# Attention, a Fourier mix and a feed-forward layer on one core: last group's sums on VectorE, last mirrored rows by an indirect store, the first row of weights in two halves of tokens, some conversions moved

## The chip, the cores and the metric

The kernel runs on one core of one Trainium2 chip. The core has engines that run their own streams of instructions in order and meet at semaphores: TensorE (PE; its weight loads are listed as PEld), VectorE (DVE), ScalarE (ACT), GpSimd (POOL) and SyncE (SP), which in this kernel only issues DMAs. ACT and POOL can issue DMAs too. Times are device microseconds of the whole execution; the metric is the median of several runs. The profile is of one execution.

## The reference

There are eight batches of 576 tokens, with eight heads of 64 numbers, so 512 numbers a token. Per batch: an attention in which the softmax of q runs over the 64 numbers of a head and the softmax of k over the tokens, then a Fourier mix, a layer norm without scale or shift, and a feed-forward layer.

```
q_s = softmax(q, over the head's numbers);  k_s = softmax(k, over the tokens)
kv  = einsum('bhsd,bhse->bhde', k_s, v);    x = einsum('bhsd,bhde->bhse', q_s, kv), heads side by side
u   = x + real(fft(fft(x, over tokens), over the 512 numbers))
un  = (u - mean(u)) / sqrt(var(u) + 1e-6)
out = u + relu(un @ w_ch1) @ w_ch2            # 512 -> 2048 -> 512
```

All is fp32. The inputs w_ch1 and w_ch2 are handed to the kernel as they are, seen as 64-bit words.

## The kernel before, in words

**Groups.** The tokens of a batch are cut in four tiles of 128, which the code names (c, u), c and u being 0 or 1; `tokens(c, u)` gives their rows. Tiles with c different from u are held in reversed order (token n and its mirror image n' are folded together for the Fourier transform, which is done by matmuls). The 64 tokens of a batch that are left over are put together over the batches in one more group, the shared one. So there are nine groups of 512 tokens, run in the order 0 to 6, the shared one, then batch 7, which is the *last group*. The place in this order is called `order`, 0 to 8.

**The feed-forward layer.** `plain` does group 0 by ordinary matmuls: `up(f)` (L1160) computes one *row* of 128 of the 2048 hidden numbers from the normalised tokens `unT` and row f of the first weights, `relu(f)` (ACT, L1165) follows, and then `part` (L1172) multiplies into the outputs. The other groups use Strassen's seven products: `up` (L1234) with its combinations `plus` (L1204: `u2` and `u3`), `other` (L1245, L1246) and `a_side` (L383 to L386, three sums of 128x512 on POOL per pair of rows), then from order 2 on `deep_down`, in which products are split once more: `a_step` (L1306) makes the combinations of the hidden tiles of a unit of two products (three on VectorE, the fourth, o = 6, on POOL), `product` (L1360) the matmuls, `ends` (L1367 and others) puts them together with temporaries `s1`, `u2`, `u3`, `into` and `sums` (L1310, L1313, POOL) add results to x, and `single` (L1330) with `add` (L1341) does products without a split. In the last group a single product, unit 4, comes at the very end and its two halves c = 0 and 1 are added to x one after the other.

**Words to weights.** The weights come as pairs of 32-bit halves, and each row of 128x512 is put together on the core by `convert(i)`: ACT scales the high half into a PSUM bank (L375), VectorE shifts it (L369) and sets the sign (L372), ACT scales the low half (L376), POOL adds (L377). Word i is row i of the first weights for i under 16, of the second after that. The banks are `bc`, `bb`, `bc`, `bb` for words 0 to 3, and `acc` later; `ba`, `bb` and `bc` are also the banks in which `up` accumulates its rows.

**Queries.** `q_exp` takes the maximum (L760), the exponential with its reduction (L766), the sum (L783), a small constant (L784), the reciprocal (L785) and scales (L794, VectorE); `q_turn` transposes on TensorE (L822) and ACT copies to qT (L832); `q_times_kv` multiplies (L884) and ACT copies the result to x (L901). The leftover tokens of two batches make a query tile of their own, named "t". `norm` normalises (L1096 on VectorE, L1099 on ACT), transposes (L1105) and copies to unT (L1114).

**Order of the work.** It is written by hand. Every step carries a planned time; all steps are sorted by it and issued in that order under a manual schedule, and each engine runs what it got in that order. The opening, up to the first normalised tokens, is a table of such times (OPENING), with WARM for products on TensorE that compute nothing that is used (L241). `first` = 46.9 is where row 0 starts in planned time. From order 1 on planned times are multiplied by 0.87. A planned time is a place in the order, not a moment in the execution.

**Stores.** `store` writes a tile of 128 tokens, or with d given one half of its 512 columns, to the output: with c equal to u by a direct DMA (L1482); with c different from u (the reversed tiles) in two steps, to a scratch tile in DRAM (L1489) and `wait` planned units later from there to the output in reversed order of rows, by pieces of 64 numbers (L1491, 256 bytes). Whole tiles and those with c = 1 leave by SP's queue, half tiles with c = 0 by ACT's.

## Time and profile before

| what | us |
|---|---|
| median of 3 runs (lowest to highest) | 1080.59 (1079.89 to 1081.19) |
| the profiled execution, whole | 1081.36 |
| its span on the core | 1079.6 |
| TensorE busy | 1059.0 |
| VectorE busy | 666.7 |
| GpSimd busy | 459.9 |
| ScalarE busy | 403.4 |
| first matmul of row 0 (L1160) starts | 51.33 |
| first matmul of row 1 starts | 55.28 |
| last matmul (L1330) ends | 1072.0 |
| last sum (L1341) starts | 1072.02 |
| last store (L1482 on SP's queue) is issued | 1072.47 |

The granted TensorE clock is 0.996 of full speed in the mean. Lines such as "PE bb L1160" name the engine, the tile written and the line of the kernel. In the list of waits the three numbers are microseconds in all, times, and the longest one. In the timeline each line is a run of like instructions: start, length from the first's start to the last's end, engine, line, operation, tiles written and read, how many, and in brackets how long the engine stood idle before and who ended it. "SPq" and "ACTq" are the DMA-issuing instructions of SP and ACT.

The sums on POOL by group of instructions: L383 (the first of the three in `a_side`) runs 32 times at 1278 ns, L1310 (`into`) 52 times at 1317 ns, L1306 on POOL 26 times at 1594 ns; L1306 on VectorE runs 92 times at 944 ns.

### The profile page before, as it was taken

How to read it: one execution, taken by the hardware profiler on the slowest of the kernel's cores; microseconds unless marked ns; L12 is line 12 of the kernel's file. 1: busy time of each engine (PE TensorE's matmuls, PEld its weight loads, DVE VectorE, ACT ScalarE, POOL GpSimd, SP SyncE). 2: the span in 40 equal slices, each digit the busy share in tenths (PEclk: the TensorE clock that was granted, in tenths of full speed). 3: DMA queues.
4: the chain of work that ended last, by engine and by line, in shares of the span. 5: the costliest groups of instructions: out<-in, count | busy, mean ns of one | idle time of the engine just before them, and what ended most of it. 6: DMA issues, size and time to landing. Idle time of an engine off the chain costs nothing.

```text
span 1079.6 us, 16993 instructions
## 1 busy us (share of the span) xinstructions
PE 1059.0 (98%) x6390; PEld 920.7 (85%) x6390; DVE 666.7 (62%) x1288; ACT 403.4 (37%) x953; POOL 459.9 (43%) x377
## 2 busy tenths in 40 slices
PE   8999999999999999999999999999999999999997
PEld 7744555988898899889998998889988998899896
DVE  6887787675545774677555765687457742562251
ACT  4675533542245215531453234522552132131200
POOL 3162220165512733454515443374236443553343
PEclk9999999999999999999999999999999999999999
DMA  9487569548976576646755577547644664665473
GB/s 338 160 283 253 176 227 308 184 171 272 341 253 206 191 254 231 223 175 200 271 177 188 195 245 239 188 178 253 216 166 161 230 238 153 234 237 203 166 247 124
DMA packets 114785, 236.29 MB, mean 219 GB/s; under 512 B 24320, under 2 KB 76160, under 8 KB 104080
## 3 DMA queue, kind: packets, MB, share of 16 engines
q1 hardware_dynamic: 112904, 234.16, 63.2%
q10 hardware_dynamic: 1800, 1.05, 0.3%
q8 instruction: 51, 0.84, 0.3%
q14 instruction: 30, 0.25, 0.1%
HBM read 200.05 MB, written 39.32 MB: 222 GB/s over the span
## 4 chain that ended last, share of the span: by engine, by line
PE 84%; DVE 3%; ACT 2%; POOL 1%; issue 1%; DVEq 0%; ACTq 0%; POOLq 0%
PE bb L1234 15%; PE bb L1360 10%; PE bc L1234 10%; PE ba L1234 10%; PE bc L1360 6%; PE ba L1360 6%; PE bb L1330 5%; PE acc L716 2%; PE acc L884 2%; PE bc L1172 2%; PE bb L1445 2%; PE acc L997 2%; PE acc L1000 2%; PE acc L1025 1%; PE bc L1445 1%; PE ba L1445 1%
## 5 line engine op out<-in xcount | busy, mean ns | idle before, releaser
L1234 PE MATMUL bb<-unT,big 128*128 128x256 f32 x768 | 183.9, 379 | 0.0
L383 POOL TENSOR_TENSOR big<-big 128x512 f32<-128x512 f32 x32 | 40.9, 1278 | 286.7 <-ACT big L1246 286.7
L1234 PEld LDWEIGHTS bb<-unT,big 128*128 128x128 f32 x768 | 142.8, 190 | 18.6 <-DVE u L1204 0.4
L1246 ACT ACTIVATE big<-big 128x512 f32<-128x512 f32 x96 | 60.4, 629 | 199.8 <-DVE big L1245 199.5
L1204 DVE TENSOR_TENSOR u<-bb,s 128x512 f32<-128x512 f32 x66 | 45.6, 691 | 132.4 <-PE bb L1234 116.0
L1234 PE MATMUL bc<-unT,big 128*128 128x256 f32 x512 | 124.0, 379 | 0.0
L1234 PE MATMUL ba<-unT,big 128*128 128x256 f32 x512 | 123.8, 379 | 0.0
L1360 PE MATMUL bb<-big 128*128 128x128 f32 x848 | 105.2, 275 | 2.2 <-DVE u L1367 2.2
L1234 PEld LDWEIGHTS ba<-unT,big 128*128 128x128 f32 x512 | 94.7, 190 | 12.4 <-issue 0.5
L1234 PEld LDWEIGHTS bc<-unT,big 128*128 128x128 f32 x512 | 94.4, 190 | 12.3 <-DVE big L1245 1.0
L1360 PEld LDWEIGHTS bb<-big 128*128 128x128 f32 x848 | 99.6, 192 | 2.9 <-DVE u L1367 2.9
L1306 DVE TENSOR_TENSOR big<-big 128x512 f32<-128x512 f32 x92 | 82.9, 944 | 5.9 <-POOL big L384 3.4
L1310 POOL TENSOR_TENSOR x<-x,big 128x512 f32<-128x512 f32 x52 | 68.0, 1317 | 28.0 <-ACT big L1337 14.8
L1360 PE MATMUL ba<-big 128*128 128x128 f32 x640 | 79.6, 275 | 0.0
L1360 PEld LDWEIGHTS ba<-big 128*128 128x128 f32 x640 | 76.3, 192 | 1.2
L766 ACT ACTIVATE q<-q,qm 128x64 f32<-128x64 f32 x248 | 67.1, 338 | 26.7 <-DVE qm L760 21.4
L1306 POOL TENSOR_TENSOR big<-big 128x512 f32<-128x512 f32 x26 | 41.2, 1594 | 74.2 <-DVE big L1306 64.0
L1367 DVE TENSOR_TENSOR u<-bb,s 128x256 f32<-128x256 f32 x40 | 16.9, 423 | 70.5 <-PE bb L1360 61.8
L1330 PE MATMUL bb<-big 128*128 128x256 f32 x256 | 58.7, 380 | 0.0
L1245 DVE TENSOR_TENSOR big<-bc,u 128x512 f32<-128x512 f32 x64 | 44.0, 687 | 23.7 <-PE bc L1234 22.6
L1330 PEld LDWEIGHTS bb<-big 128*128 128x128 f32 x256 | 48.2, 190 | 8.0 <-DVE big L1245 1.1
L1360 PE MATMUL bc<-big 128*128 128x128 f32 x416 | 51.5, 275 | 0.0
(254 smaller groups left out, 2017.2 us busy)
## 6 DMA issues: line engine op xcount, KB each, us to landing
big<-w2d SPq DMA_DIRECT2D x67, 1024.0 KB, 4.8
big<-w1s SPq DMA_DIRECT2D x64, 896.0 KB, 4.8
big<-w2s SPq DMA_DIRECT2D x16, 1024.0 KB, 6.4
big<-in_w_dram SPq DMA_DIRECT2D x21, 512.0 KB, 6.2
w2d<-big SPq DMA_DIRECT2D x42, 256.0 KB, 5.4
q<-in_q_dram SPq DMA_DIRECT2D x28, 256.0 KB, 6.4
k<-in_kT_dram SPq DMA_DIRECT2D x24, 288.0 KB, 6.0
v<-in_v_dram SPq DMA_DIRECT2D x24, 256.0 KB, 4.8
```

Source lines behind the costliest of these rows:

```text
L383: e1.tensor_tensor(out=to(4), in0=at(2), in1=at(3), op=ALU.add)
L716: nc.tensor.matmul(pk, lhsT=ks[:, c, :], rhs=v[:, c, :], start=(c == 0), stop=(c == NC - 1))
L766: nc.scalar.activation(q[:, h, :], q[:, h, :], ACT.Exp, bias=m[:, h:h + 1])
L1204: plus = lambda t: V.tensor_tensor(out=temp(t), in0=box["bb"][:], in1=box["s1"][:], op=ALU.add)
L1234: nc.tensor.matmul(bank()[:, i, :], lhsT=w[:, WA_AT[m], k * P:(k + 1) * P], rhs=self.unT[g][:, B_AT[m], k, :], start=first and i == 0 and ...
L1245: steps = [(0, lambda: V.tensor_tensor(out=hp(i), in0=bank()[:], in1=u()[:], op=ALU.add)), (0.8, lambda: nc.scalar.activation(hp(i), hp(i) ...
L1246: (0.8, lambda: nc.scalar.activation(hp(i), hp(i), ACT.Relu))]
L1306: e.tensor_tensor(out=to(o), in0=to(x), in1=to(y), op=op)
L1310: G.tensor_tensor(out=x, in0=x, in1=tile(m), op=ALU.add)
L1330: nc.tensor.matmul(box[name][:, i, :], lhsT=h[p][:, A_AT[m], i * P:(i + 1) * P], rhs=self.stream[n][:, p, :], start=p == 0 and (m != 1 or ...
L1360: nc.tensor.matmul(box[place[n]][:, i, :], lhsT=own(m)(A_AT[n])[:, f, :], rhs=w[:, r // 2, r % 2 * P:r % 2 * P + P], start=first and f == ...
L1445: nc.tensor.matmul(bank()[:, i, :], lhsT=h[p][:, A_AT[m], i * P:(i + 1) * P], rhs=w[:, p, :], start=first and i == 0 and p == 0, stop=p == ...
```

## The change

1. **First row of weights.** `plain` computes row 0 in two halves of tokens, each 256 columns wide, into the same bank: `half(0)` at planned time -0.9 and `half(1)` at 0 from the row's start. The ReLU of row 0 is placed at 2.5, not 3.5. The last pair of warm-up products is dropped from WARM. Word 3's high half goes to `acc`, not `bb`, and word 2 is placed 0.5 later (1.4 after the first word's place at 0.3). The scaling by k1's inverse moves from 51.0 to 53.0.
2. **Conversions and queries.** In the second half of group 0 three words are placed later (5.5, 9, 12 become 7.2, 10, 13), the second query tile's product with kv 0.8 later. In `attention_timed` the products with kv move from 11.7 to 12.1 after their query, and the inverse of the "t" query from 5.5 to 4.8.
3. **deep_down.** For all groups but the last, the a_steps of units after the first come 3 planned units later, except where the plan has `t - n + 2`.
4. **The last group.** `a_side`, the fourth a_step, `into` and `sums` run on VectorE; the three last `into` are placed at 0.6, 1.2, 1.8 after the last unit, not 1, 2, 4.
5. **Last stores.** The reversed tiles of the last three stores go straight to the output by an indirect DMA of POOL, for which a tile `row` of 128 numbers, made by iota 20 planned units ahead, gives each partition its row. They are the second column half of the tile (1, 0), and the tile (0, 1), whose two column halves were stored apart before and now go whole after the first of unit 4's sums. Stores are declared independent of stores in other queues.

```diff
-WARM = (3, 3), (24.7, 6), (41.9, 2), (43.45, 1), (44.5, 1), (45.5,2)
+WARM = (3, 3), (24.7, 6), (41.9, 2), (43.45, 1), (44.5, 1)
...
-45.47 turn11, 45.62 laid10, 46.22 laid11, 51.00 k1 inverse, 51.30 k1 scale0, 51.60 k1 scale1"""
+45.47 turn11, 45.62 laid10, 46.22 laid11, 53.00 k1 inverse, 53.30 k1 scale0, 53.60 k1 scale1"""
...
-            n = ("bc", "bb", "bc", "bb")[i] if i < 4 else "acc"
+            n = ("bc", "bb", "bc")[i] if i < 3 else "acc"
...
-            steps += at(t, self.q_exp(it)) + at(t + 8.7, self.q_turn(it)) + at(t + 11.7, self.q_times_kv(it))
+            steps += at(t, self.q_exp(it)) + at(t + 8.7, self.q_turn(it)) + at(t + 12.1, self.q_times_kv(it))
...
-        return [(0, top)] + [(0.8 + h / 2, lambda h=h: exps((h, h + 1))) for h in range(0, H, 2)] + [(5.5, inverse)]
+        return [(0, top)] + [(0.8 + h / 2, lambda h=h: exps((h, h + 1))) for h in range(0, H, 2)] + [(4.8 if it[0] == "t" else 5.5, inverse)]
...
+        def half(c):
+            if c == 0:
+                down[0, "h"] = self.ps.tile([P, 512], F32, tag="ba", name="ba")
+            cols = slice(c * P, (c + 1) * P)
+            for k in range(KT):
+                nc.tensor.matmul(down[0, "h"][:].rearrange("p (u n) -> p u n", u=2)[:, :, cols],
+                                 lhsT=self.w1sb[:, 0, k * P:(k + 1) * P], rhs=unT()[:, k // 2 * 2:k // 2 * 2 + 2, k % 2, cols],
+                                 start=(c == 0 and k == 0), stop=(k == KT - 1), skip_group_check=True)
...
+        first[0] = [(-0.9, lambda: half(0)), (0, lambda: half(1)), (2.5, lambda: relu(0))]
...
-        base = self.base[order]
+        base, e = self.base[order], V if order == B else nc.gpsimd
...
-                        steps.append((1.6, lambda: self.a_side(hp, hp, nc.gpsimd, nc.gpsimd)))
+                        steps.append((1.6, lambda: self.a_side(hp, hp, e, e)))
...
+        E = V if last else G
...
-                           6: (1, 5, G, ALU.subtract)}[o]
+                           6: (1, 5, E, ALU.subtract)}[o]
...
-            G.tensor_tensor(out=x, in0=x, in1=tile(m), op=ALU.add)
+            E.tensor_tensor(out=x, in0=x, in1=tile(m), op=ALU.add)
...
-            G.tensor_tensor(out=result[m], in0=result[m], in1=result[k], op=ALU.add)
+            E.tensor_tensor(out=result[m], in0=result[m], in1=result[k], op=ALU.add)
...
-                 (5, 3): [(1, into, 1, 1, 5), (2, into, 0, 1, 5), (4, into, 0, 1, 3)]}
+                 (5, 3): [(0.6, into, 1, 1, 5), (1.2, into, 0, 1, 5), (1.8, into, 0, 1, 3)] if last else
+                         [(1, into, 1, 1, 5), (2, into, 0, 1, 5), (4, into, 0, 1, 3)]}
...
-                    half(t - 3.7 + 4 * c, c, unit // 4, 0)
+                    if unit == 4 and c == 0:
+                        steps.extend(self.scatter(t - 3.7, g, c, 1, lambda: self.xpart(g, 0, 1)))
+                    else:
+                        half(t - 3.7 + 4 * c, c, unit // 4, 0)
...
-            early = 6 if last and t < n + 8 else 0 if t == 8 else t - n + 2 if i == 2 else t - n
+            early = 6 if last and t < n + 8 else 0 if t == 8 else t - n + 2 if i == 2 else t - n + (0 if last else 3)
...
-            for c in range(2):
-                half(t - 8 + 3.5 + c, c, 1, 1)
-                half(t - 8 + 6.5 + c, c, 0, 1, 0.7 if c else 9)
+            half(t - 8 + 2, 1, 1, 1)
+            half(t - 8 + 3, 0, 0, 1)
+            steps.extend(self.scatter(t - 8 + 3.1, g, 1, 0, lambda: self.xs[g, 0][:, 1, HD:], 1))
...
+    def apart(self, store):
+
+        for name in {"sync", "scalar", "gpsimd"} - {of := self.queue(store)}:
+            self.tc.declare_no_dep(store.ins, group=name, reason="each store of rows has rows of its own")
+        self.tc.add_to_no_dep_group(of, store.ins)
...
+    def scatter(self, t, g, c, u, x, d=None):
+
+        nc, n = self.nc, 1 if d is None else 2
+        rows = self.out.rearrange("b s (e n) -> (b s e) n", e=n)
+        box = []
+
+        def index():
+            box.append(self.small.tile([P, 1], I32, tag="row", name="row", bufs=2))
+            nc.gpsimd.iota(box[0][:], pattern=[[0, 1]], base=n * (g * S + tokens(c, u).stop - 1) + (d or 0), channel_multiplier=-n)
+
+        def there():
+            to = bass.IndirectOffsetOnAxis(ap=box[0][:, 0:1], axis=0)
+            self.apart(nc.gpsimd.indirect_dma_start(out=rows, out_offset=to, in_=x(), in_offset=None))
+
+        return [(t - 20, index), (t, there)]
...
-            return [(0, lambda: e.dma_start(out, x()))]
+            return [(0, lambda: self.apart(e.dma_start(out, x())))]
...
-        return [(0, there), (wait, lambda: e.dma_start(cols(out)[:, ::-1, :], cols(box[0])))]
+        return [(0, there), (wait, lambda: self.apart(e.dma_start(cols(out)[:, ::-1, :], cols(box[0]))))]
...
-    words = [first + 0.3, *(first + 0.9 + 1.7 * i for i in range(NF - 2))]
-    words += [first + dt for dt in (27, 31, 35, 39, 44, 49)] + [t + dt for dt in (-2, 2, 5.5, 9, 12, 26, 30, 33, 36, 39)]
+    words = [first + 0.3, first + 1.4, *(first + 0.9 + 1.7 * i for i in range(1, NF - 2))]
+    words += [first + dt for dt in (27, 31, 35, 39, 44, 49)] + [t + dt for dt in (-2, 2, 7.2, 10, 13, 26, 30, 33, 36, 39)]
...
-        steps += at(at_q + 9.5, blk.q_turn(it)) + at(at_q + 14, blk.q_times_kv(it))
+        steps += at(at_q + 9.5, blk.q_turn(it)) + at(at_q + 14 + 0.8 * (i == 1), blk.q_times_kv(it))
```

More of the change, by code (lines that the diff above doesn't have):

```diff
@@ L356, in convert @@
             out = (self.w1sb if i < NF else self.w2sb)[:, f, :]
-            n = ("bc", "bb", "bc", "bb")[i] if i < 4 else "acc"
+            n = ("bc", "bb", "bc")[i] if i < 3 else "acc"
             if i < 26:
-                t = self.ps.tile([P, 512], F32, tag=n, name=n, bufs=3 if i >= 4 else 1)[:]
+                t = self.ps.tile([P, 512], F32, tag=n, name=n, bufs=3 if i >= 3 else 1)[:]
             else:
@@ L1468, in down, with queue @@
                                                   (2, 2): out(1, 1, False), (1, 2): out(0, 1, True)}, early)
+    def apart(self, store):
+        for name in {"sync", "scalar", "gpsimd"} - {of := self.queue(store)}:
+            self.tc.declare_no_dep(store.ins, group=name, reason="each store of rows has rows of its own")
+        self.tc.add_to_no_dep_group(of, store.ins)
+    def queue(self, store):
+        return {"SP": "sync", "Activation": "scalar", "Pool": "gpsimd"}[str(store.ins.engine).split(".")[-1]]
+    def scatter(self, t, g, c, u, x, d=None):
[9 more added lines that the diff above has]
+        return [(t - 20, index), (t, there)]
     def store(self, g, c, u, x, d=None, wait=9):
```

## The prediction

> **What bounds the kernel.** First the page: span, busy engines, shares of the chain that ended last.
>
> ```profile
> span 1079.6 us, 16993 instructions
> PE 1059.0 (98%) x6390; PEld 920.7 (85%) x6390; DVE 666.7 (62%) x1288; ACT 403.4 (37%) x953; POOL 459.9 (43%) x377
> PE 84%; DVE 3%; ACT 2%; POOL 1%; issue 1%; DVEq 0%; ACTq 0%; POOLq 0%
> ```
>
> TensorE works 98% of the span and is 84% of the chain. So time can be had in three places: matmuls taken out, the few idle spots between them, and what follows the last one. The waits of TensorE list the spots (us in all, times, longest):
>
> ```profile
> PE bb L1360 <- DVE u L1367: 2.2, 2, 1.6
> PE tr L822 <- DVE q L794: 1.8, 3, 1.1
> PE acc L884 <- ACT qT L832: 1.2, 3, 0.9
> PE tr L1105 <- ACT unT L1114: 0.4, 1, 0.4
> PE bb L1160 <- DVE big L372: 0.3, 1, 0.3
> ```
>
> The end, from the chain of waits and then the timeline (start, us, what, idle before):
>
> ```profile
> 1068.53 3.47 PE bb L1330 x16
> ```
> ```profile
> 1065.71 3.83 POOL L1310 TENSOR_TENSOR x<-x,big 128x512 f32<-128x512 f32 x3 [6.13 <-DVE big L1367]
> 1070.03 2.16 ACTq L1491 DMA_DIRECT2D out_dram<-mirror  x2
> 1071.43 0.67 SPq L1491 DMA_DIRECT2D out_dram<-mirror  x1
> 1072.02 0.43 DVE L1341 TENSOR_TENSOR x<-bb,x 128x256 f32<-128x256 f32 x1 [2.96 <-PE bb L1330]
> 1072.47 2.04 SPq L1482 DMA_DIRECT2D out_dram<-x  x1
> ```
>
> and from the windows (stretch, PE, PEld, DVE, ACT, POOL, clock, DMA share, GB/s):
>
> ```profile
> 1077.00:1078.00 1.00, 0.00 (x0) 0.00 (x0) 0.00 (x0) 0.00 (x0) 0.00 (x0) 0.50 0.30 77
> 1078.00:1079.60 1.60, 0.00 (x0) 0.00 (x0) 0.00 (x0) 0.00 (x0) 0.00 (x0) 0.50 0.02 5
> ```
>
> The last matmul ends at 1072.0; 7.6 us follow with no engine at work, only stores. The DMA packets tell why: each of the three reversed copies (L1491) is 512 packets of 256 B and takes 2.6 to 3.5 us (1071.67-1074.31, 1073.93-1077.4, 1074.96-1077.94). The last store, issued at 1072.47, has its data among them, 1075.03 to 1078.28; the span ends 1.27 us later.
>
> **What the Trainium skill says.** "DMA: Bandwidth & Descriptors", section "Anatomy of one DMA — SWDGE (gpsimd) path", prices a store issued by GpSimd at 2.0 us + bytes/436e3; the trace has no such store, so nothing here confirms it. "SBUF — State Buffer", "Who interferes with whom": VectorE and GpSimd share a port pair under an exclusive lock. The trace agrees: L1306 on VectorE takes 0.68 alone and 1.43 to 1.75 beside a GpSimd sum. "VectorE: DVE Perf Modes" gives an fp32 tensor_tensor of 512 elements as 691 ns; here 0.68 to 0.69. The same sum on GpSimd (L1310 in the last group) is 1.27.
>
> **1. First row in halves of tokens.** The timeline shows the warm-up products (L241), row 0, and row 1's wait:
>
> ```profile
> 50.04 1.03 PE L241 MATMUL ba<-kvr,ident 128*128 128x256 f32 x4
> 51.33 3.67 PE L1160 MATMUL ba<-unT,big 128*128 128x512 f32 x8 [0.26 <-PE ba L241]
> 52.98 2.54 POOL L377 TENSOR_TENSOR big<-big 128x512 int32<-128x512 int32 x2 [8.79 <-DVE big L372]
> 55.28 3.67 PE L1160 MATMUL bb<-unT,big 128*128 128x512 f32 x8 [0.28 <-DVE big L372]
> ```
>
> The row keeps its matmul work (twice as many instructions, half the columns). The warm-up at 50.04 (0.86 us) goes, and half 0 needs only tokens laid by 49.31, so it starts near 50.04. Half 1 needs the copies ending 50.39 and 50.93 and follows at about 51.77, ending near 53.5. Row 1, in bank bb, waited for word 3, whose high half stands in bb until its sign is taken (L372, 54.47 to 55.13); word 3 now goes to acc. What is left for row 1 is word 1 itself: VectorE now does both of its operations (0.68 each) ahead of word 2's, so POOL's add (1.29, from 52.98 before) starts near 52.5 and ends near 53.8. Row 1 starts near 53.85, not 55.28: a lead of 1.4. The k1 inverse moved from 51 to 53 is not read before the attention of batch 1: nothing.
>
> Is the lead kept? ACT and VectorE work of batch 1 is fed by DMA and by converted words, not by TensorE, so TensorE runs into it. L884 at 113.13 already waits for the qT of 112.50-113.08; one L1172 (0.86) now runs ahead of it, so of 1.4 about 0.9 survives. Then words 24 and 25 are put later (5.5 to 7.2, 9 to 10), so L783, L784, L785, L794 pass two conversions of VectorE (0.69 each, twice) and end near 119.2, not 121.85; the 1.26 us wait of L822 goes: lead 2.1. But the norm transpose L1105 at 166.77 stands 0.15 us behind ACT L1099, which hangs on a VectorE lane without a hole from here:
>
> ```profile
> 155.47 0.42 DVE L427 TENSOR_TENSOR spare<-big 128x256 f32<-128x256 f32 x1 [2.77 <-DMA w2s<-spare]
> ```
>
> That waits for a store back and a load on SP's queue, and I make its own lead about 0.85, from L945 (127.55) ahead of it. I keep 1.0 of the 2.1, between 0.5 and 2.1.
>
> **2. Tail queries of batches 4 and 6.** L794 feeds L822 late, twice alike:
>
> ```profile
> 436.81 0.69 DVE L794 TENSOR_TENSOR q<-q,qrec 128x512 f32<-128x512 f32 x1
> 437.56 0.66 PE L822 MATMUL tr<-ident,q 128*128 128x128 f32 x4 [0.37 <-DVE q L794]
> ```
>
> From matmul start to matmul start, against the usual cadence, this costs 0.53 (436.81 and 668.88). With the inverse at 4.8 VectorE does it ahead of an L760 and two L724, 1.2 us earlier: gone. L884 (445.19, 677.25) costs 0.32 or 0.33; at 12.1 it stands behind half a product more (0.86): gone. 2 x (0.53 + 0.32) = 1.7.
>
> **3. The last unit's a_steps 2.6 us later, orders 2 to 7.** u2 (L1367) is now behind one L1306, not four: the waits of L1360 at 395.05, 627 and 859.86 go, 0.23 + 0.23 + 0.83 = 1.3. But u3 comes behind four L1306, of which two run beside POOL (1.43 and 1.75 in the trace, not 0.68). u3's slack was 0.38 in orders 3 and 5 (398.73, 630.79) and like it in order 6, over 1.1 in 2 and 4. I charge 0.25 for each of 3 and 5 and 0.2 for the rest: 0.7. Net 0.6, from -0.3 (u3 late by 0.5 in three orders) to 1.3. The other wait of L1360, 1.6 us at 943.7, keeps its order and stays.
>
> **4. Last group's sums on VectorE.** Four times three a_side operations, one each 0.6 after the other: u2 of L1204 comes about 0.6 later, with 0.78 of slack (995.01 is the tight one): nothing, and if that cover is gone a few tenths three times. The last three L1310 take 3 x 0.66 on VectorE, 1065.57 to 1067.55, not until 1069.54 on POOL. L1341 of ba at 1068.64 comes after them. Stores can leave 2 us sooner.
>
> **5. The last stores.** Out go three pairs L1489 and L1491: three of 128 KB to the scratch and 1536 packets of 256 B. In come two index operations 20 steps earlier on an idle POOL (nothing) and two indirect stores of POOL: 128 rows of 1 KB ready at 1067.55, 128 rows of 2 KB ready at 1069.06. By the price of the skill the second needs 2.6 us, so 1071.7, or about 1073 if they go one after the other: under the cover of the last product (1072.0) and the last store. On SP and ACT one direct store each is ahead (1066.3, 1067.6), long away. So the last SP store (1072.47) has an empty machine. The like store at 1067.00 had its last packet 1.6 us after issue: 1074.1, plus 1.27 is 1075.3, against 1079.56: 4.2. Bounds: 1.5 if building descriptors on POOL costs several us; 4.5 if the end after the last packet is shorter. The declared independence of stores in different queues frees only waits on stores long done: nothing.
>
> **Sum.** 1.0 + 1.7 + 0.6 + 0.0 + 4.2 = 7.5. Span 1079.6 becomes 1072.1; the profiled execution (1081.36, 1.8 of it outside the span) 1073.9. It lies 0.8 above the median shown, so the median goes from 1080.59 to 1073.1.
>
> **Rivals.** (a) *The indirect stores come last.* Both are 256 rows built one after the other from 1067.55. They stay hidden up to 25 ns a row (landed 1074); at 40 ns they land at 1077.8 and the tail gives 1.5 to 2: 1075.7. For it: no row shows such a store. Against: the skill's price, 2.6 us for the larger. (b) *The lead is eaten.* The VectorE lane at 155-166 and the ACT copies of qT are full, and u3 is late in all orders: parts 1 and 3 give 0.5 - 0.3, with parts 2 and 5 6.1: 1074.5. For it: slacks of 0.15 and 0.38. Against: the waits removed are in the list. (c) *Everything is kept*, 2.1 + 1.7 + 1.3 + 4.5 = 9.6: 1071.0. (d) *Slower.* The tail's place is taken by POOL's stores: without the tail's 4.2 the sum is 3.3, so the two must last past 1079.6 + 3.3 on this scale to cost anything and 2.2 more to be seen, 17.5 us for 256 rows, 68 ns a row, six times the price. For it only that the operation is unseen; POOL idles then, so nothing delays it further. That the change doesn't do what it says is a part of (a): the last store no longer waits behind small packets, but POOL's 256 KB.
>
> **Chances and range.** 0.2% is 2.2 us, about what a measurement of this kernel can tell from no change. The forecast 0.50, (a) 0.20, (b) 0.15, (c) 0.10, (d) and unseen losses of its kind 0.05. Range 1070.6 (c, with 0.4 for noise) to 1077.6 (a with b's losses, at 3 us of gain). Faster 0.93, same 0.02, slower 0.05; all cases but (d) lie over 2.2 us below.
>
> **What would show it.** Right: no wait of L1160 on L372; row 1 near 53.9; no waits of L822 or L884 in orders 3 and 5; L1360 after u2 only in order 7; last matmul about 3.3 us earlier, near 1068.7; 3.4 us from it to the end, the last packets those of an SP store. Wrong: L1105 with a new wait near 166 (part 1); waits of L1360 on u3 beside POOL sums (part 3); L1360 or L1234 of the last group waiting for VectorE sums (part 4); packets of POOL's queue after the last store's (part 5), which above all would spoil the number.

## The result, and the profile after

The changed kernel takes 1073.05 us in the median of 4 runs (1072.76 to 1073.53), against 1080.36 (1079.89 to 1081.19, 4 runs) before. The ratio is 0.9932, 95% interval 0.9915 to 0.9949: 7.3 us, 0.7% less. The forecast was 1073.1. Its sum came out nearly exactly, but by luck: of its four terms only one came out near its size, and the errors of the others cancel.

The page of the changed kernel begins so (span, busy engines, shares of the chain that ended last):

```profile
span 1071.0 us, 16992 instructions
PE 1058.3 (99%) x6394; PEld 922.4 (86%) x6394; DVE 685.9 (64%) x1317; ACT 404.8 (38%) x953; POOL 422.5 (39%) x352
PE 84%; DVE 3%; ACT 2%; issue 1%; POOL 1%; DMA 0%; POOLq 0%; DVEq 0%; ACTq 0%
```

VectorE has 19 us more work, POOL 37 us less, TensorE the same. `a_side`, by the way, makes four sums (L383 to L386), not three as was said above. The lines of the code have moved: L1244 is the up product (L1234 before), L1214 its u2 and u3, L1371 the split product (L1360), L1378 its ends (L1367), L1317 the a_steps (L1306), L1321 `into` (L1310), L1341 and L1352 the last products and their sums (L1330, L1341), L1522 the direct store (L1482), L1506 the indirect one. Experiments that leave lines out stand up to three lines higher.

The waits of TensorE behind the first 36 us (us in all, times, longest):

```profile
PE bb L1371 <- DVE u L1378: 1.8, 2, 1.6
PE bb L1244 <- DVE u L1214: 0.8, 2, 0.4
PE tr L1105 <- ACT unT L1114: 0.5, 1, 0.5
PE bb L1160 <- POOL big L377: 0.2, 1, 0.2
```

The six waits on the queries are gone (two in group 0, four in orders 3 and 5), and that of L1160 on L372. The one of L1244 on L1214 is new, in orders 3 and 5. Not shown here, nor in the prediction's list, are the waits ahead of 36 us (L241, L537, L997), which no edit touches: 6.7 us before and 5.0 now.

The first row, from the timeline:

```profile
49.20 3.62 PE L1169 MATMUL ba<-unT,big 128*128 128x256 f32 x16
51.68 2.62 POOL L377 TENSOR_TENSOR big<-big 128x512 int32<-128x512 int32 x2 [8.30 <-DVE big L372]
53.02 3.70 PE L1160 MATMUL bb<-unT,big 128*128 128x512 f32 x8 [0.19 <-POOL big L377]
```

Both halves run without a hole, and row 1 waits 0.19 us for its own word, nothing else.

The end, from the timeline, and two pieces of the chain of waits:

```profile
1060.55 2.02 DVE L1321 TENSOR_TENSOR x<-x,big 128x512 f32<-128x512 f32 x3
1062.60 0.37 ACTq L1522 DMA_DIRECT2D out_dram<-x  x1
1063.28 3.62 PE L1341 MATMUL bb<-big 128*128 128x256 f32 x16
1063.48 0.42 DVE L1352 TENSOR_TENSOR x<-ba,x 128x256 f32<-128x256 f32 x1 [0.90 <-PE ba L1341]
1063.49 1.17 POOL L1506 DMA_INDIRECT out_dram<-x,row  x1 [86.18 <-DMA out_dram<-x]
1066.92 0.97 POOL L1506 DMA_INDIRECT out_dram<-x,row  x1 [2.26 <-DMA out_dram<-x,row]
1066.93 0.42 DVE L1352 TENSOR_TENSOR x<-bb,x 128x256 f32<-128x256 f32 x1 [3.03 <-PE bb L1341]
```
```profile
1063.49 2.61 DMA out_dram<-x,row
1066.70 1.19 POOLq L1681
```

The last matmul ends at 1066.9; 4.1 us follow, where there were 7.6. The second indirect store's tile was ready at 1063.9 (the sum at 1063.48), but it starts at 1066.92: POOL waited for the first one to land (1063.49 + 2.61). In the packets the last SP store is done at 1068.8 and the second indirect store at 1069.5, so the indirect one is last.

**A ledger.** The matmuls of the two profiles are the same ones in the same order, but for row 0 and the warm-up, so the start of each can be subtracted from its like. The difference is constant over long stretches and changes only at a few places:

| stretch | changed kernel earlier by, us | step |
|---|---|---|
| 14 to 48 us | 0.84 | 0.84 |
| from row 1 (53 us) | 2.23 | 1.39 |
| from the product L884 near 112 us | 3.07 | 0.84 |
| from the transpose L822 near 119 us | 3.95 | 0.88 |
| at 170 and 300 us | 3.90 | -0.05 |
| after order 2's last unit (395 us) | 4.03 | 0.13 |
| after order 3's queries (450 us) | 4.35 | 0.32 |
| after order 4's last unit (627 us) and order 5's queries (700 us) | 4.83 | 0.48 |
| after order 6's last unit (900 us) | 5.22 | 0.39 |
| in the last group (from 1000 us) | 5.09 | -0.13 |
| end of the span | 8.59 | 3.50 |

The profiles differ by 8.6 us and the medians by 7.3. The first step explains most of that: nothing in the first 48 us was edited. The prediction put the waits of L1360 at 395 and 627 us, and the u3 at 398.73 and 630.79, into orders 3 and 5, and one expectation below does so too; the times are right, but they lie in orders 2 and 4.

Kernels with the same instructions up to 45 us stand between 0.6 us ahead of the changed kernel's profile and 1.9 behind it, for two reasons. The first waits on ACT (L537 near 7 to 10 us) differ in length. And TensorE runs at a slow pace for a time: its matmuls take 0.42 us each up to 11.6 us in the changed kernel's profile, up to 12.7 in that of before and up to 14.7 where opening and words are put back (below), and 0.28 after that (those of L559 are the same matmuls on both sides); in the last kernel below those of L559 take 0.28 from the first on. In the profile of before the granted clock on record is 0.50 from 9.3 to 12.7 us; in the changed kernel's the record begins only at 11.65, with 1.00. Where opening and words are put back, the waits make 0.74 us of the 1.9 and the slow stretch the rest. So below a shift is counted from its value between 14 and 48 us. The step at 112 us is in part of the same kind: where the instructions are those of the changed kernel, L884 lost between 0.2 and 1.0 us there against its usual pace.

### The profile page after: what moved, and what is told of

Its sections match the earlier page's. It is cut to its first block, busy times and chain, and to the rows that moved or that the text cites. A ratio compares the mean times of both kernels' runs of the same rounds, so it can differ in the third digit from the quotient of the medians.

```text
span 1071.0 us, 16992 instructions
## 1 busy us (share of the span) xinstructions
PE 1058.3 (99%) x6394; PEld 922.4 (86%) x6394; DVE 685.9 (64%) x1317; ACT 404.8 (38%) x953; POOL 422.5 (39%) x352
## 4 chain that ended last, share of the span: by engine, by line
PE 84%; DVE 3%; ACT 2%; issue 1%; POOL 1%; DMA 0%; POOLq 0%; DVEq 0%; ACTq 0%
PE bb L1244 15%; PE bb L1371 10%; PE bc L1244 10%; PE ba L1244 10%; PE bc L1371 6%; PE ba L1371 6%; PE bb L1341 4%; PE acc L716 2%; PE acc L884 2%; PE bc L1181 2%; PE bb L1460 2%; PE acc L997 2%; PE acc L1000 2%; PE acc L1025 2%; PE bc L1460 1%; PE ba L1460 1%
## 5 line engine op out<-in xcount | busy, mean ns | idle before, releaser
L1244 PE MATMUL bb<-unT,big 128*128 128x256 f32 x768 | 184.4, 380 | 0.8 <-DVE u L1214 0.8
L1244 PEld LDWEIGHTS bb<-unT,big 128*128 128x128 f32 x768 | 142.5, 190 | 20.3 <-DVE u L1214 2.3
L383 POOL TENSOR_TENSOR big<-big 128x512 f32<-128x512 f32 x28 | 35.9, 1281 | 255.9 <-ACT big L1256 255.9
L1244 PE MATMUL ba<-unT,big 128*128 128x256 f32 x512 | 123.8, 379 | 0.0
L1244 PE MATMUL bc<-unT,big 128*128 128x256 f32 x512 | 123.5, 380 | 0.0
L1214 DVE TENSOR_TENSOR u<-bb,s 128x512 f32<-128x512 f32 x66 | 45.6, 691 | 117.7 <-PE bb L1244 97.4
L1371 PE MATMUL bb<-big 128*128 128x128 f32 x848 | 105.2, 275 | 1.8 <-DVE u L1378 1.8
L1244 PEld LDWEIGHTS bc<-unT,big 128*128 128x128 f32 x512 | 94.7, 190 | 12.5 <-DVE big L1255 1.0
L1244 PEld LDWEIGHTS ba<-unT,big 128*128 128x128 f32 x512 | 94.4, 190 | 12.2 <-issue 0.5
L1371 PEld LDWEIGHTS bb<-big 128*128 128x128 f32 x848 | 99.6, 192 | 2.2 <-DVE u L1378 2.2
L1321 POOL TENSOR_TENSOR x<-x,big 128x512 f32<-128x512 f32 x45 | 57.7, 1297 | 62.7 <-issue 32.9
L1317 DVE TENSOR_TENSOR big<-big 128x512 f32<-128x512 f32 x94 | 78.1, 875 | 2.5 <-POOL big L386 2.5
L1371 PE MATMUL ba<-big 128*128 128x128 f32 x640 | 79.6, 275 | 0.0
L1371 PEld LDWEIGHTS ba<-big 128*128 128x128 f32 x640 | 76.3, 192 | 1.2
L1341 PE MATMUL bb<-big 128*128 128x256 f32 x256 | 58.7, 380 | 0.0
L1378 DVE TENSOR_TENSOR u<-bb,s 128x256 f32<-128x256 f32 x40 | 16.8, 421 | 64.6 <-PE bb L1371 59.9
L1341 PEld LDWEIGHTS bb<-big 128*128 128x128 f32 x256 | 48.2, 190 | 8.0 <-DVE big L1255 1.1
L1371 PE MATMUL bc<-big 128*128 128x128 f32 x416 | 51.5, 275 | 0.0
L1371 PEld LDWEIGHTS bc<-big 128*128 128x128 f32 x416 | 48.9, 192 | 0.0
```

What stands on the lines that cost most here:

```text
L383: e1.tensor_tensor(out=to(4), in0=at(2), in1=at(3), op=ALU.add)
L1214: plus = lambda t: V.tensor_tensor(out=temp(t), in0=box["bb"][:], in1=box["s1"][:], op=ALU.add)
L1244: nc.tensor.matmul(bank()[:, i, :], lhsT=w[:, WA_AT[m], k * P:(k + 1) * P], rhs=self.unT[g][:, B_AT[m], k, :], start=first and i == 0 and ...
L1317: e.tensor_tensor(out=to(o), in0=to(x), in1=to(y), op=op)
L1321: E.tensor_tensor(out=x, in0=x, in1=tile(m), op=ALU.add)
L1341: nc.tensor.matmul(box[name][:, i, :], lhsT=h[p][:, A_AT[m], i * P:(i + 1) * P], rhs=self.stream[n][:, p, :], start=p == 0 and (m != 1 or ...
```

## The experiments

Medians of one kernel scatter by about 1 us, so where a step is under 1.5 us the matmul shifts of the profiles carry the verdict and the medians only must not contradict. Every median stands beside its own runs of before on the same chip.

### The old stores, with the sums on VectorE

```diff
-                    if unit == 4 and c == 0:
-                        steps.extend(self.scatter(t - 3.7, g, c, 1, lambda: self.xpart(g, 0, 1)))
-                    else:
-                        half(t - 3.7 + 4 * c, c, unit // 4, 0)
+                    half(t - 3.7 + 4 * c, c, unit // 4, 0)
...
-            half(t - 8 + 2, 1, 1, 1)
-            half(t - 8 + 3, 0, 0, 1)
-            steps.extend(self.scatter(t - 8 + 3.1, g, 1, 0, lambda: self.xs[g, 0][:, 1, HD:], 1))
+            for c in range(2):
+                half(t - 8 + 3.5 + c, c, 1, 1)
+                half(t - 8 + 6.5 + c, c, 0, 1, 0.7 if c else 9)
```

> The changed kernel with the three last reversed stores as before (scratch tile, then reversed copy in 256-byte pieces), the last group's sums still on VectorE. Theory (the small pieces make the tail): the time from the last matmul to the end of the span, 4.1 us in the changed kernel, grows to 6.3 to 7.6 us, the last SP store again has its data among 256-byte packets, and the median rises by 2.2 to 3.5 us. Rival (what shortened the tail is that the sums ended 2 us sooner on VectorE): the tail stays at 5 us or less, median up by under 1 us.

Measured: 1074.51 us (1074.19 to 1077.06, 5 runs) against 1080.58, ratio 0.9944 (0.9930 to 0.9957). In its profile the last matmul ends at 1069.01 and the span at 1075.17: 6.16 us, 2.1 more than with the new stores and just under the theory's 6.3, well over the rival's 5. Its timeline and its windows (stretch, PE, PEld, DVE, ACT, POOL, clock, DMA share, GB/s):

```profile
1066.96 3.38 ACTq L1528 DMA_DIRECT2D out_dram<-mirror  x2
1069.50 0.34 SPq L1519 DMA_DIRECT2D out_dram<-x  x1
```
```profile
1071.00:1072.00 1.00, 0.00 (x0) 0.00 (x0) 0.00 (x0) 0.00 (x0) 0.00 (x0) 0.89 0.31 77
1072.00:1073.00 1.00, 0.00 (x0) 0.00 (x0) 0.00 (x0) 0.00 (x0) 0.00 (x0) 0.50 0.31 76
```

The DMA engines go at 77 GB/s with the 256-byte pieces, as before. The three reversed copies follow one another, 1067.9 to 1070.0, 1070.0 to 1071.8, 1072.1 to 1074.0, and the SP store's packets (1070.4 to 1072.2) stand among them. The last data here is a reversed copy's. The SP store's own data end 2.7 us after its issue; in the kernel before it was 5.8 (1072.47 to 1078.28), in the changed one it is 1.4 (1067.4 to 1068.8). So the copies hold it up by 1.3 us here, and then set the end themselves. The experiment swaps the whole detour. Each copy closes with 4 packets of 4 bytes, each direct store of the end with 16, and the DMA share of 0.31 is that of about five of the 16 engines, so a copy seems to run on few engines only. Whether the size of the pieces, these few engines or the second trip through DRAM costs the time is not shown.

### The old sums, with the new stores

The first kernel puts the three L1321 back on POOL at their old places.

```diff
-        E = V if last else G
+        E = G
...
-                 (5, 3): [(0.6, into, 1, 1, 5), (1.2, into, 0, 1, 5), (1.8, into, 0, 1, 3)] if last else
-                         [(1, into, 1, 1, 5), (2, into, 0, 1, 5), (4, into, 0, 1, 3)]}
+                 (5, 3): [(1, into, 1, 1, 5), (2, into, 0, 1, 5), (4, into, 0, 1, 3)]}
```

(and `a_side` in the same way.)

> The changed kernel with the last group's sums back on POOL, at the places in the plan that they had before; the indirect stores stay. Theory (the second indirect store waits for the first one's landing, and the first waits for these sums): the first indirect store starts about 1.8 us later against the last matmul, the second follows it by the same 3.4 us, and the span ends 1.3 to 1.9 us later. Rival (the sums are hidden, the last SP store sets the end): under 0.3 us later.

Measured: 1073.46 us (1072.76 to 1074.84) against 1080.58. It doesn't answer the question: the new stores stand at 3 and 3.1 of the plan, ahead of the third sum at 4, so two halves left without it, and the output lacks that sum there. The second kernel puts the two behind it:

```diff
-            half(t - 8 + 3, 0, 0, 1)
-            steps.extend(self.scatter(t - 8 + 3.1, g, 1, 0, lambda: self.xs[g, 0][:, 1, HD:], 1))
+            half(t - 8 + 4.05, 0, 0, 1)
+            steps.extend(self.scatter(t - 8 + 4.1, g, 1, 0, lambda: self.xs[g, 0][:, 1, HD:], 1))
```

> The changed kernel with the last group's sums on POOL at their old places and the last stores placed behind them. Theory (indirect stores come one after the other, and the first waits for the sums): the first indirect store starts 1.5 to 2.2 us later against the last matmul, the second 1.3 to 2.2 us later, and the span ends 1.3 to 2.0 us later than in the changed kernel against the last matmul. Rival (the sums' place is covered by the last product): under 0.4 us later.

Measured: 1073.41 us (1073.15 to 1075.29, 4 runs) against 1079.98, ratio 0.9941 (0.9924 to 0.9958). Its timeline:

```profile
1060.13 3.83 POOL L1321 TENSOR_TENSOR x<-x,big 128x512 f32<-128x512 f32 x3 [6.11 <-DVE big L1378]
1064.26 1.17 POOL L1505 DMA_INDIRECT out_dram<-x,row  x1 [0.30 <-POOL x L1321]
1067.66 0.97 POOL L1505 DMA_INDIRECT out_dram<-x,row  x1 [2.23 <-DVE x L1352]
```

The last matmul ends at 1066.41. The first indirect store starts 2.15 us ahead of that, where it was 3.40 ahead; the second 1.25 us after it, where it was 0.03 after; the span ends 5.07 us after it, not 4.08. So the direction is the theory's and each size is less: 1.25, 1.22 and 0.99 us, where 1.5, 1.3 and 1.3 were its lower bounds. The sums do end 1.87 us later against the last matmul (2.45 us ahead of its end, where it was 4.32), but the store starts 0.30 us behind POOL's own sum, and 0.92 us behind VectorE's in the changed kernel (1062.57 to 1063.49). The rival's 0.4 is out. In the other direction POOL's sums won 0.13 us in the last group (the shift goes from -0.35 to -0.48 near 990 us): the four sums of `a_side` on VectorE do delay a u2, as the ledger's last step but one has it.

The two experiments make a table of the time after the last matmul:

| | old stores | new stores |
|---|---|---|
| sums on POOL | 7.58 (before) | 5.07 |
| sums on VectorE | 6.16 | 4.08 (changed) |

Each cell is one profile; in five other kernels below that end like the changed one it is 4.06 to 4.08. The stores are worth 2.1 to 2.5 us, the sums 1.0 to 1.4.

### One indirect store left out

```diff
-            steps.extend(self.scatter(t - 8 + 3.1, g, 1, 0, lambda: self.xs[g, 0][:, 1, HD:], 1))
```

> The changed kernel without its first indirect store: the second column half of the tile (1, 0) of the last batch isn't written, so a part of the output is left out. Theory (the second indirect store is late because it waits for the first one to land, and it is what ends the span): it now starts about 2 us ahead of the end of the last matmul instead of beside it, its packets come ahead of the last SP store's, and from the last matmul to the end it takes 3.0 to 3.4 us instead of 4.1; median down by 0.5 to 1.1 us. Rival (the last SP store sets the end already): the time after the last matmul stays at 3.9 to 4.2 us.

Measured: 1072.33 us (1071.82 to 1073.87, 4 runs) against 1079.98, ratio 0.9925 (0.9908 to 0.9941). The one store that is left:

```profile
1066.61 1.18 POOL L1505 DMA_INDIRECT out_dram<-x,row  x1 [87.58 <-DMA out_dram<-x]
```

Its sum ends at 1065.7, the last matmul at 1068.69: it starts 2.1 us ahead of that end, its packets are through at 1069.2, the SP store's at 1070.5, and the span ends 3.41 us after the last matmul. The theory holds, at the upper edge. What the line names as releaser, a DMA to the output, is the profile's inference; the 0.92 us from the sum to the start are the same in the changed kernel (1062.57 to 1063.49) and in the last kernel below, where the sum itself is named as releaser (1058.61 to 1059.53). So this looks like a delay of POOL behind another engine's sum, and not like a wait for the direct store.

### The words of group 0 back

```diff
-    words += [first + dt for dt in (27, 31, 35, 39, 44, 49)] + [t + dt for dt in (-2, 2, 7.2, 10, 13, 26, 30, 33, 36, 39)]
+    words += [first + dt for dt in (27, 31, 35, 39, 44, 49)] + [t + dt for dt in (-2, 2, 5.5, 9, 12, 26, 30, 33, 36, 39)]
...
-        steps += at(at_q + 9.5, blk.q_turn(it)) + at(at_q + 14 + 0.8 * (i == 1), blk.q_times_kv(it))
+        steps += at(at_q + 9.5, blk.q_turn(it)) + at(at_q + 14, blk.q_times_kv(it))
```

> The changed kernel with the three words at 5.5, 9, 12 and the second query's product at its old place. Theory (TensorE keeps every lead it gets up to the end of group 0; moving the words was worth 1.7 us): matmuls agree with the changed kernel up to 110 us, waits of L822 on VectorE and L884 on ACT come back near 111 to 119, and from there to the end matmuls are 1.4 to 1.9 us later; median up by as much. Rival (the recorded one: a VectorE lane hung on a DMA at 155 us takes the lead in any case): behind 170 us the matmuls are later by under 0.5 us.

Measured: 1074.40 us (1073.26 to 1075.48, 5 runs) against 1080.58, ratio 0.9942 (0.9928 to 0.9956). The waits of its TensorE:

```profile
PE tr L822 <- DVE q L794: 1.1, 1, 1.1
PE acc L884 <- ACT qT L832: 1.0, 1, 1.0
```

Matmuls are 0.94 us later from 112 us, 1.82 from 119, and 1.33 behind 170 us: the norm transpose L1105 gives back 0.5 there, its wait on ACT is not in the list any more. So 1.3 us stay, just under the theory's 1.4 to 1.9, of which up to 0.9 is the wait of L884 that comes and goes. The words themselves are worth 0.4 to 1.3 us.

### The first row whole

```diff
-        first[0] = [(-0.9, lambda: half(0)), (0, lambda: half(1)), (2.5, lambda: relu(0))]
...
-            n = ("bc", "bb", "bc")[i] if i < 3 else "acc"
+            n = ("bc", "bb", "bc", "bb")[i] if i < 4 else "acc"
```

(with the warm-up pair, the k1 inverse and word 2's place as before.)

> The changed kernel with the first row of weights whole, the warm-up pair, the old banks and the old place of word 2. Theory (the lead of row 1 is kept whole): matmuls from row 1 on are 1.4 to 1.6 us later, and still 1.3 to 1.6 us later at 170 us and at the end; median up by as much. Rival (the recorded step: the lead is spent at the query's product near 111 us and at the norm near 166): 1.4 us later at row 1 but under 0.6 us later behind 170 us.

Measured: 1074.46 us (1073.19 to 1075.88, 5 runs) against 1080.58, ratio 0.9943 (0.9929 to 0.9956). Row 1 is 1.39 us later, to the hundredth what the ledger shows; 0.3 of it comes back at the norm (L1105 waits less), and 0.99 us is left at the end. That is short of the theory's 1.3 and far over the rival's 0.6.

```profile
PE bb L1160 <- DVE big L372: 0.3, 1, 0.3
PE ba L1160 <- PE ba L241: 0.3, 1, 0.3
```

### Row and words back together

Both edits above in one kernel:

```diff
-        first[0] = [(-0.9, lambda: half(0)), (0, lambda: half(1)), (2.5, lambda: relu(0))]
...
-(-2, 2, 7.2, 10, 13, 26, 30, 33, 36, 39)
+(-2, 2, 5.5, 9, 12, 26, 30, 33, 36, 39)
```

> The changed kernel with both the opening (whole first row, warm-up, banks) and the words of group 0 as before. Counted from the matmuls of 12 to 40 us, and with the wait of L884 on qT near 111 us taken out, which differs between executions: theory (the two parts add, as they were measured one by one, 1.2 and 0.45): 1.4 to 2.0 us later than the changed kernel at the end. Rival (what the profiles of before and after show side by side is due to the edits, 2.3 or more): 2.2 to 3.2 us later. The recorded 1.0 with its bounds 0.5 to 2.1 holds in the first case and falls in the second.

Measured: 1075.27 us (1074.72 to 1078.00, 5 runs) against 1079.88, ratio 0.9953 (0.9939 to 0.9966). From 14 to 48 us it is 1.92 us behind the changed kernel's profile, at the end 5.14: 3.22, and without the 0.82 of L884, 2.4. The rival holds: together the two parts are worth more than one by one (1.0 + 0.4).

```profile
PE tr L822 <- DVE q L794: 1.1, 1, 1.1
PE acc L884 <- ACT qT L832: 0.9, 1, 0.9
PE tr L1105 <- ACT unT L1114: 0.5, 1, 0.5
```

The last line says where the difference lies: alone, either part's loss was partly swallowed by the norm's wait near 166 us; with both back that wait stands in full. Why ACT's copies are as late again with both was not tried.

### The queries of batches 4 and 6 back

```diff
-            steps += at(t, self.q_exp(it)) + at(t + 8.7, self.q_turn(it)) + at(t + 12.1, self.q_times_kv(it))
+            steps += at(t, self.q_exp(it)) + at(t + 8.7, self.q_turn(it)) + at(t + 11.7, self.q_times_kv(it))
...
-[(4.8 if it[0] == "t" else 5.5, inverse)]
+[(5.5, inverse)]
```

> The changed kernel with the products with kv at 11.7 and the leftover queries' inverse at 5.5 again. Theory (the waits removed, 0.85 us an order, were mostly replaced by a wait of the up product on u behind VectorE's folding of the leftover queries, 0.59): in orders 3 and 5 the waits of L822 and L884 come back, that of L1244 on L1214 goes, and matmuls are 0.2 to 0.35 us later behind each, 0.4 to 0.7 us at the end. Rival (the recorded 1.7 us was gained, and the new waits come from elsewhere): 1.5 us or more later at the end, with the new waits still there.

Measured: 1073.65 us (1072.89 to 1074.85, 4 runs) against 1079.98, ratio 0.9936 (0.9919 to 0.9952). Matmuls are 0.32 us later behind order 3's queries and 0.35 behind order 5's, 0.65 at the end. The waits come back and that of L1244 is gone:

```profile
PE tr L822 <- DVE q L794: 0.7, 2, 0.4
PE acc L884 <- ACT qT L832: 0.3, 2, 0.2
```

What took the rest shows in the timeline of the changed kernel:

```profile
437.42 1.28 DVE L784 TENSOR_SCALAR qrec<-qrec 128x8 f32<-128x8 f32 x1
440.18 0.54 DVE L857 TENSOR_TENSOR T<-F 128x120 f32<-128x120 f32 x1
440.63 0.68 DVE L1214 TENSOR_TENSOR u<-bb,s 128x512 f32<-128x512 f32 x1
441.37 1.13 PE L1244 MATMUL bb<-unT,big 128*128 128x256 f32 x4 [0.42 <-DVE u L1214]
```

The u3 of L1214 stands behind the folding of the leftover queries (L854 to L857). Before, its matmul came 0.85 us later and found it ready; now TensorE is early and loses 0.58 against its usual pace, in both orders.

### The a_steps back

```diff
-t - n + (0 if last else 3)
+t - n
```

> The changed kernel with the a_steps of the last unit at their old places in orders 2 to 7. Theory (the later places took away the waits on u2 and brought next to none on u3): the waits on u2 come back, 0.15 to 0.3 us in orders 3 and 5 and 0.6 to 0.9 us in order 6, and matmuls are 0.6 to 1.3 us later at the end. Rival (the recorded charge: u3 pays back 0.7): 0.6 us later or less, and waits of L1371 in the changed kernel on u3 near the last unit go.

Measured: 1073.75 us (1072.36 to 1074.19, 4 runs) against 1079.98, ratio 0.9935 (0.9919 to 0.9952).

```profile
PE bb L1371 <- DVE u L1378: 2.2, 2, 1.6
```

Matmuls are 0.13 us later from order 2's last unit (395 us), 0.15 from order 4's (627), 0.39 from order 6's (859), 0.67 in all: the theory's lower edge. No wait on u3 is in the list of the changed kernel, but a short one is in its trace: in orders 2 and 4 the lead falls by 0.09 us right behind the last unit's u3, with the a_steps later and not with them back. So of the rival's payback of 0.7 there came 0.2; that the total is near the forecast's is a coincidence of two errors.

### Four more moves

The readings above name four waits that an order on an engine makes. This kernel moves the four:

```diff
-            steps += at(21 if start < 0 else 35, self.t_fold(it))
+            steps += at(22.2 if start < 0 else 35, self.t_fold(it))
...
-        base, e = self.base[order], V if order == B else nc.gpsimd
+        base, e = self.base[order], V if order >= B - 1 else nc.gpsimd
...
-        E = V if last else G
+        E, late = V if last else G, 4 if order == B - 2 else 3
...
-t - n + (0 if last else 3)
+t - n + (0 if last else late)
...
-                 (5, 3): [(0.6, into, 1, 1, 5), (1.2, into, 0, 1, 5), (1.8, into, 0, 1, 3)] if last else
+                 (5, 3): [(0.6, into, 0, 1, 5), (1.2, into, 0, 1, 3), (1.8, into, 1, 1, 5)] if last else
...
-            half(t - 8 + 2, 1, 1, 1)
-            half(t - 8 + 3, 0, 0, 1)
-            steps.extend(self.scatter(t - 8 + 3.1, g, 1, 0, lambda: self.xs[g, 0][:, 1, HD:], 1))
+            half(t - 8 + 3, 1, 1, 1)
+            half(t - 8 + 2, 0, 0, 1)
+            steps.extend(self.scatter(t - 8 + 2.1, g, 1, 0, lambda: self.xs[g, 0][:, 1, HD:], 1))
```

The second is aimed at the largest wait that was left, in the shared group. The changed kernel's timeline there:

```profile
931.14 1.26 POOL L386 TENSOR_TENSOR big<-big 128x512 f32<-128x512 f32 x1
932.44 5.68 DVE L1317 TENSOR_TENSOR big<-big 128x512 f32<-128x512 f32 x4 [2.50 <-POOL big L386]
938.04 0.41 DVE L1378 TENSOR_TENSOR u<-bb,s 128x256 f32<-128x256 f32 x1
938.51 1.72 PE L1371 MATMUL bb<-big 128*128 128x128 f32 x13 [1.59 <-DVE u L1378]
```

VectorE waits 2.5 us for POOL's last a_side sum, then makes four a_steps at 1.4 us each beside other sums of POOL, and u2 comes after them.

> The changed kernel with four more moves: the folding of the leftover queries behind the up product's u in orders 3 and 5; the shared group's a_side sums on VectorE; the a_steps of order 6 one unit later; and, at the end, the sums into the half that is stored by the first indirect store ahead of the third sum. Theory (each of the waits seen in the changed kernel is an order on one engine, and nothing else stands right behind it): the waits of L1244 on u (0.58 twice), of L1371 on u in order 7 (1.75) and in order 6 (0.41) go, and from the last matmul to the end it takes 3.4 to 3.7 us instead of 4.1. In all 3.2 to 3.9 us less than the changed kernel, a median of 1069.1 to 1069.9. Rival (as with the products with kv, another engine's lane stands right behind and takes most of it): under 2 us in all.

Measured: 1069.12 us (1068.58 to 1069.28, 4 runs) against 1079.88 (9 runs), ratio 0.9895 (0.9880 to 0.9910): 10.8 us less than before, 3.9 less than the median of the changed kernel. None of the waits on u is left in the list. Behind 170 us the matmuls gain 0.50 in order 3, 0.48 in order 5, 0.39 in order 6, 1.85 in the shared group, 3.3 with small change; the time after the last matmul is 3.74 us (0.04 over what was expected). The chain now ends in TensorE and the last sum:

```profile
1060.08 3.47 PE bb L1341 x16
1063.57 0.42 DVE x L1352
```

and from its timeline, the first indirect store:

```profile
1057.19 2.02 DVE L1321 TENSOR_TENSOR x<-x,big 128x512 f32<-128x512 f32 x3
1059.53 1.17 POOL L1506 DMA_INDIRECT out_dram<-x,row  x1 [85.57 <-DVE x L1321]
```

The last SP store's packets end at 1065.7, after those of the second indirect store (1065.3).

## Why the prediction was right, and where it was not

| step | forecast, us | measured, us | by |
|---|---|---|---|
| 1, opening and group 0 | 1.0 | 2.4 | row and words back together |
| 2, queries of batches 4 and 6 | 1.7 | 0.6 | queries back |
| 3, a_steps later | 0.6 | 0.7 | a_steps back |
| 4 and 5, last sums and stores | 4.2 | 3.4 | 3.50 after the last matmul, less 0.13 in the last group |
| sum | 7.5 | 7.1 | medians: 7.3 |

That 7.1 lies so near 7.5 is luck: the errors are +1.4, -1.1, +0.1 and -0.8 us. The profiles' 8.6 us are about this 7.1, and 0.84 of opening and about 0.8 of L884, which differ between executions. The sign "last matmul about 3.3 us earlier" came out at 5.1 in the profiles, about 3.5 without these two; from it to the end it takes 4.1 us, not 3.4, and the last packets are not an SP store's.

**What bounds the kernel** was read rightly: TensorE nearly without holes, so that only holes and the tail could give time. All of the 7.3 us came from there.

**Step 1, mis-sized.** Row 1's lead was forecast as 1.4 and is 1.39, and row 1 itself, at 53.02 in a profile that was 0.84 early, is where it was put (53.85). The step that failed is "I keep 1.0 of the 2.1": that the norm near 166 us would cap the lead at about 0.85 to 1. The 2.4 lie outside the bounds given there, 0.5 to 2.1. The norm does take part of a lead when only one of the edits is made, 0.3 or 0.5 us, but not with both: there its wait is as long in the changed kernel (0.5 in the list) as with the opening put back. The VectorE lane that hangs on the DMA at 155.47 moved along: the same L427, with the same 2.77 us of idle time ahead of it, is at 151.54 in the changed kernel, 3.93 us earlier, and so is the norm's L1099 (165.80 to 161.88). A lane that waits for a DMA isn't fixed in time when what issues the DMA moves.

**Step 2, failed in its core.** "Gone ... 2 x (0.53 + 0.32) = 1.7" took the waits off and did not ask what is late next. The waits did go, but the u3 of the up product, behind the folding on the same VectorE, was less than 0.85 us ahead of its matmul (0.85 less the new 0.58, so about 0.3), and two thirds of the gain turned into that wait. Moving the folding behind u3 gave 0.5 us in each order.

**Step 3, right in sum by two errors.** The u2 waits gave about 0.85, not 1.3 (order 6 keeps 0.41 of its 0.8), and of u3's payback of 0.7 only 0.2 came, 0.09 in each of orders 2 and 4; 0.67 is what is left.

**Steps 4 and 5.** That the reversed copies hold the last store was right, and the new stores are worth 2.1 to 2.5 us; that it is the size of the pieces is not shown. Three things were wrong. The sums were costed as nothing of their own, though they bring 1.0 to 1.4 of the 3.5, since the first store waits for them. The sentence "to 1071.7, or about 1073 if they go one after the other" had the second case, which is what happens, and called it covered: the second store's end was put 1 us ahead of the last SP store's and came 0.8 us behind it, because it starts only when the first has landed and POOL takes 0.8 us more to begin. Why the second waits for that landing is not shown; the kernel declares only stores of different queues independent, and these two leave by one. And `a_side` on VectorE is not free: 0.13 us.

**The rivals.** Rival (a) named the right event, that the indirect stores come last, by the wrong mechanism: no slow building of rows, but one store waiting for the other's landing; it cost 0.7 us, not 2.5. Rival (d) needed 17.5 us for the two; they took 6.0, from 1063.5 to 1069.5. Its "six times the price" counts the two as one store of 384 KB; for two the price that it uses gives 2.3 + 2.6, and 17.5 us is 3.6 times that.

**The skill's pages.** The price in "DMA: Bandwidth & Descriptors", section "Anatomy of one DMA — SWDGE (gpsimd) path", 2.6 us for 256 KB and 2.3 for 128 KB, counts the completion in. From start to landing the trace has 3.0 and 2.6, so 0.3 to 0.4 more; the last packets are through after 2.6 and 2.3.

## What to carry to other kernels

When a wait on a busy engine is removed, look up how far ahead of its reader the *next* result in that engine's queue is: here the gain was about that slack, 0.3 us of 0.85. Two indirect stores of one queue to one tensor came one after the other here, with a full landing between them, so put the data of the first of them first, or make them one (not tried here). And before crediting a profile pair with a difference, look at a stretch that nobody edited: here it held 0.8 us, and part of that is a slow stretch of TensorE in the first 15 us that ends earlier or later in each execution.

## What the runs showed of the hardware that was not expected

A VectorE instruction of eight elements a partition, L784, takes 0.17 us in the median and up to 1.28 beside a POOL sum:

```profile
L784 DVE TENSOR_SCALAR qrec<-qrec x32: 171/172/1281, 19.8 to 804.5; 128x8 f32<-128x8 f32 x32
```

(name, then minimum, median and maximum in ns.) The Trainium skill, "SBUF — State Buffer", section "Who interferes with whom", says that a tensor_scalar can take both ports, and that then the engine that comes second is blocked until the other is done. The trace agrees: eight of the 32 take 0.53 to 1.28 us, and each of them ends within 0.05 us after the end of a POOL sum (1.27 long). So a tiny instruction can cost a chain a whole POOL sum, and here it stood in the very lane that L1214 was late in. It stays at 1.28 there with the folding moved, where L1244 waits no more, so the folding's place was enough.

An indirect store of 256 KB took only 0.35 us more from start to last data than one of 128 KB: in the changed kernel 1063.49 to 1065.75 in packets for the first and 1066.92 to 1069.53 for the second. After the last packet 1.2 to 1.6 us pass until the span ends in the six profiles looked at, with an indirect store last (1069.53 to 1070.97) as with a direct one (1065.70 to 1067.27) or a reversed copy (1074.01 to 1075.17).
